# Relu² attention and a mixture-of-depths FFN on one core: batch 2's loads before the expert weights, and scatter-adds and row stores issued later

## Chip, cores and metric

The kernel runs on one core of a Trainium2 chip. The metric is the device time of one execution in microseconds, the median of the runs. The profile is of one further execution, whose span from the first to the last instruction was 249.8 us.

## What is computed

For 8 batches of 12 heads, 448 positions and head size 64, attention with a squared relu in place of softmax: `relu(q kᵀ / 8)² / 448` times `v`. The heads of a position, side by side, are its row `x` of 768 numbers. Then a gate `score = x · w_gate` picks the 128 highest positions of each batch, and only those rows go through a feed-forward layer:

```python
top_idx = np.argpartition(-scores[b], capacity)[:capacity]
xe = x[b, top_idx]
h = np.maximum(xe @ w1, 0.0)          # w1: 768 x 1024
ye = h @ w2                           # w2: 1024 x 768
g = 1.0 / (1.0 + np.exp(-scores[b, top_idx]))
out[b, top_idx] = x[b, top_idx] + g[:, None] * ye
```

All other rows of `out` are `x` itself. All inputs and the output are float32 in device memory; the kernel works in bfloat16.

## The kernel before

**Loop.** One loop runs over 48 steps `t`, one for each pair of heads; batch `b` has the six steps `hp` = 0 to 5. A step transposes q and k of the next pair on TensorE (`transposes`, L165 and L171; copied out by VectorE at L176), makes scores in four chunks (L186, L190), applies relu on ScalarE (L198) and squares on VectorE (L204), multiplies the step before with `v` (`attend`, L214), and copies that result to `xT` (`evacuate`, L223 or L225). From `xT` a DMA transpose on SyncE's queue (L229) fills `x_sb[b]`, the rows of the batch.

**The second half runs behind the first.** In batch `b` the steps also carry, for batch `b-1`, the gate scores and the ranking (`moe_rank`: scores L257, rank compare L280 against the constant `tie`, one-hot L285 against `slot_row`, gather L296), and, for batch `b-2`, the feed-forward layer (`moe_ffn`: h L329, y L345, the gated result `gye` L350). `chosen` (L305 to L307) copies the selected token numbers to the tile `idx`; for batch `b` it stands at the first step of batch `b+2`. `idx` and `gye` have two buffers each, `x_sb` two, the q, k and v buffers three.

**Order of work.** The loop stands under a manual schedule: each engine runs its instructions in the order in which the loop writes them. What stands ahead of the loop (first loads, constants) is placed by the scheduler, mostly in the order of the text.

**Transfers on GpSimd's (POOL's) queue.** All loads convert float32 to bfloat16 and are issued by GpSimd. `load(b)` is nine transfers: one of q (L79), four of k and four of v (L88, L91), together 4.1 MB read. Ahead of the loop come `load(0)` in parts, `load(1)`, three iotas that make `slot_row`, `tie` and the token numbers (L131, L137, L144), and the weights w1 and w2 (L152, L153; 3.1 MB each). Within the loop, `load(b+2)` stands at the first step of batch `b`; then the store of the rows of batch `b-1` (L233) follows from `evacuate`; and at the fifth-numbered step (`hp` = 5) `gated` calls the scatter-add of batch `b-2` (`scatter`, L384), an indirect DMA that adds 128 rows of `gye` into `out` at the positions in `idx`. Stores and scatter-adds of any batch write the same tensor `out`, and each of one kind waits for the one of the other kind issued before it.

Of the kernel before, what the change touches and what calls it, by code (L numbers as in the profile page):

```python
# [19 lines left out]
def kernel(  # L20
# [11 lines left out]
    nc = tc.nc  # L32

    B, H, S, Dh = q.shape
# [3 lines left out]
    P = 112  # L38
    NC = S // P
    NM = HD // 128  # L40
    NF = F // 128
    NHP = H // 2
# [52 lines left out]
    def load(b, h0, h1):  # L95
        load_q(b, h0, h1)
        load_kv(k_sb, k, b, h0, h1)
        load_kv(v_sb, v, b, h0, h1)
# [16 lines left out]
    for i in range(1, NBUF):  # L115
        zero_halves(i)
    load(1, 0, H)
    w1_sb = const.tile([128, NM, F], BF16)
    w2_sb = const.tile([128, NF, HD], BF16)

    wg_rep = const.tile([128, NM, 128], BF16)
    nc.vector.tensor_copy(out=wg_rep,
# [26 lines left out]
        nc.vector.tensor_copy(out=t[:, :, 0:2], in_=tok_i)  # L149
        tok.append(t)  # L150

    nc.gpsimd.dma_start(out=w1_sb, in_=moe_w1.rearrange("(m p) f -> p m f", p=128))  # L152
    nc.gpsimd.dma_start(out=w2_sb, in_=moe_w2.rearrange("(m p) f -> p m f", p=128))  # L153


    qkt, s_ps, a_sb, o_ps, x_sb = {}, {}, {}, {}, {}
# [43 lines left out]
    def square(t, c):  # L200
        n = 2 if c < 3 else 1
        r = r_sb.pop((t, c))
        a = a_sb[t, c] = a_pool.tile([128, 2, S], BF16, name="a_sb")
        nc.vector.tensor_tensor(out=a[:, :n], in0=r[:, :n], in1=r[:, :n], op=ALU.mult)  # L204
# [13 lines left out]
    def evacuate(t):  # L218
        b, hp = divmod(t, NHP)
        xt = xT[b % 2][:, hp, :, :P]  # L220
        o = o_ps.pop(t).rearrange("d (c p) -> d c p", p=P)
        if hp in (0, 4, 5):
            nc.vector.tensor_scalar(out=xt, in0=o, scalar1=o_scale, scalar2=None, op0=ALU.mult)  # L223
        else:
            nc.scalar.activation(out=xt, in_=o, func=AF.Copy, scale=o_scale)  # L225
        if hp == 0:
            x_sb[b] = x_pool.tile([128, NC, HD], BF16, name="x_sb")

        nc.sync.dma_start_transpose(  # L229
            out=x_sb[b][:, :, hp * 128:(hp + 1) * 128],  # L230
            in_=xT[b % 2][:, hp].rearrange("d c p -> d (c p)"))
        if hp == NHP - 1:
            nc.gpsimd.dma_start(out=out[b].rearrange("(p c) d -> p c d", c=NC), in_=x_sb[b][:P])  # L233

# [83 lines left out]
    def moe_ffn(b, idx, g, xeT):  # L320
        hT = moe_pool.tile([128, NF, CAP], BF16, name="hT")
        gye = moe_pool.tile([CAP, HD], FP32, name="gye")
        ps = {}

        def hidden(f, pool=mb_ps_pool, tag="m"):
            if f % 4 == 0:
                ps["h", f // 4] = pool.tile([128, 4, CAP], FP32, name="h_ps", tag=tag)
            for m in range(NM):
                nc.tensor.matmul(out=ps["h", f // 4][:, f % 4, :],  # L329
                                 lhsT=w1_sb[:, m, f * 128:(f + 1) * 128],  # L330
                                 rhs=xeT[:, m, :], start=(m == 0), stop=(m == NM - 1))

        def hidden_relu(i):
            nc.scalar.activation(out=hT[:, 4 * i:4 * i + 4, :], in_=ps["h", i], func=AF.Relu)

        def sigmoid():
            nc.scalar.activation(out=g, in_=g, func=AF.Sigmoid)

        def project(half, f0, f1, pool=None, tag="m"):
            cols_d = slice(half * 384, half * 384 + 384)  # L340
            if f0 == 0:
                pool = pool or (ma_ps_pool, mb_ps_pool)[half]
                ps["y", half] = pool.tile([CAP, 384], FP32, name="ye_ps", tag=tag)
            for f in range(f0, f1):
                nc.tensor.matmul(out=ps["y", half], lhsT=hT[:, f, :], rhs=w2_sb[:, f, cols_d],  # L345
                                 start=(f == 0), stop=(f == NF - 1))

        def gated(half):
            cols_d = slice(half * 384, half * 384 + 384)
            nc.scalar.activation(out=gye[:, cols_d], in_=ps["y", half], func=AF.Copy,  # L350
                                 scale=g[:, 0:1])
            if half == 1:
                scatter()

        def last():

            nc.scalar.activation(out=g, in_=g, func=AF.Sigmoid)
            for half in range(2):
                h = s_ps_pool.tile([128, 4, CAP], FP32, name="h_ps2", tag="s")
                for m0 in (0, 3):  # L360
                    for ff in range(4):
                        f = 4 * half + ff
                        for m in range(m0, m0 + 3):
                            nc.tensor.matmul(out=h[:, ff, :],
                                             lhsT=w1_sb[:, m, f * 128:(f + 1) * 128],
                                             rhs=xeT[:, m, :], start=(m == 0 and ff == 0),
                                             stop=(m == NM - 1), skip_group_check=True)
                f = 4 * half
                nc.scalar.activation(out=hT[:, f:f + 4, :], in_=h, func=AF.Relu)
            y = [mb_ps_pool.tile([CAP, 384], FP32, name="y_ps2", tag="m"),  # L370
                 t_ps_pool.tile([CAP, 384], FP32, name="y_ps3", tag="t")]
            for f0 in (0, 4):
                for half in range(2):
                    for f in range(f0, f0 + 4):
                        nc.tensor.matmul(out=y[half], lhsT=hT[:, f, :],
                                         rhs=w2_sb[:, f, half * 384:half * 384 + 384],
                                         start=(f == 0), stop=(f == NF - 1))
            nc.scalar.activation(out=gye[:, :384], in_=y[0], func=AF.Copy, scale=g[:, 0:1])
            nc.vector.tensor_scalar(out=gye[:, 384:], in0=y[1], scalar1=g[:, 0:1],
                                    scalar2=None, op0=ALU.mult)  # L380
            scatter()

        def scatter():
            nc.gpsimd.indirect_dma_start(  # L384
                out=out.rearrange("b s d -> (b s) d"),
                out_offset=bass.IndirectOffsetOnAxis(ap=idx[:, :1], axis=0),
                in_=gye, in_offset=None, element_offset=b * S * HD, compute_op=ALU.add)

        return {"h": hidden, "hT": hidden_relu, "sig": sigmoid, "y": project, "gye": gated,
                "last": last}  # L390


# [24 lines left out]
    def moe(engine, b, hp):  # L417

        if b >= 2 and hp == 0:
            place(engine, b - 1, NHP)  # L420
        place(engine, b, hp)
# [13 lines left out]
    with tc.manual_schedule():  # L435
        transposes(0)
        for t in range(NT):
            b, hp = divmod(t, NHP)
            scores(t, 0)
            scores(t, 1)  # L440
            relu(t, 0)
            relu(t, 1)
            moe(ACT, b, hp)
            if t > 0:
                square(t - 1, 3)
            moe(DVE, b, hp)
            if t + 1 < NT:
                transposes(t + 1)
            if t > 0:
                attend(t - 1)  # L450
                if hp not in (0, 1, 5):
                    evacuate(t - 1)
            if hp == 0 and b + 2 < B:
                load(b + 2, 0, H)
            scores(t, 2)
            relu(t, 2)
            square(t, 0)
            if t > 0 and hp in (0, 1, 5):
                evacuate(t - 1)
            square(t, 1)  # L460
            moe(DVE2, b, hp)
            scores(t, 3)
            relu(t, 3)
            square(t, 2)
            moe(PE, b, hp)
        square(NT - 1, 3)
        place(ACT, B - 1, NHP)
        place(DVE, B - 1, NHP)
        last, prev = B - 1, B - 2
        r, handed[last] = moe_rank(last)  # L470
        f = moe_ffn(prev, *handed.pop(prev))
        attend(NT - 1)
        evacuate(NT - 1)
        r["gate"](0, NM - 1)
        for i in range(4):
            f["h"](i)
        r["gate"](NM - 1, NM)
        f["hT"](0)
        r["bc"]()
        for i in range(4, 8):  # L480
            f["h"](i, t_ps_pool, "t")
        r["col"]()
        r["pieces"]()
        for c in range(NC):
            r["rank"](c)
        r["hot"]()
        f["hT"](1)
        f["sig"]()
        f["y"](0, 0, 8, mb_ps_pool)
        f["y"](1, 0, 8, o_ps_pool, "o")  # L490
        f["gye"](0)
        f["gye"](1)
        r["xe"](0, t_ps_pool, "t")
        r["sel"]()
        r["xe"](1, ma_ps_pool)
        r["xeT"](0)
        r["xeT"](1)
        r["chosen"]()
        moe_ffn(last, *handed.pop(last))["last"]()
# [33 lines left out]
```

## Time and profile before

| | |
|---|---|
| time, median of 3 | 253.89 us (253.05 to 253.95) |
| span of the profiled execution | 249.8 us |
| TensorE busy | 201.2 us, 81% |
| VectorE busy | 179.9 us, 72% |
| ScalarE busy | 183.2 us, 73% |
| GpSimd busy | 83.5 us, 33% |
| moved by DMA | 40.50 MB (39.32 MB read from device memory, 14.16 MB written to it) |
| mean granted TensorE clock | 0.942 |

The page has the busy time of each engine, then the span in 40 equal slices with a digit for the busy tenths in each, then the DMA queues, the chain of work that ended last, and the costliest groups of instructions. Lines of a timeline give start, duration (both in us), engine, source line, operation, output and input, the count, and in brackets the idle time before it and what ended that. For a DMA the engine's line is only its issue; the landing is seen in who waited for it. The median time from issue to landing was 10.8 us for the row stores (L233), 5.9 us for the scatter-adds (L384), 11.7 us for the q loads and 21.7 us for the weights.

### The profile page before, as it was taken

The numbers are of one execution on the slowest core, as the hardware profiler recorded it, in microseconds if no ns is written. First come the engines' busy times: TensorE is split into PE (matmuls) and PEld (weight loads), VectorE is DVE, ScalarE is ACT, GpSimd is POOL, SyncE is SP. The second block draws the span as 40 slices with busy tenths as digits, with TensorE's granted clock in tenths as the row PEclk, the third lists the DMA queues.
The fourth block names the chain that finished last, engine by engine and source line by source line (L and its number), as shares of the span: only waits on it lengthen the run. The fifth ranks groups of instructions, "written<-read, shape, count | busy, mean of one in ns | idle before, by whom it ended". The sixth has DMA issues, their size and how long they took to land.

```text
span 249.8 us, 5910 instructions
## 1 busy us (share of the span) xinstructions
PE 201.2 (81%) x2304; PEld 115.5 (46%) x2304; DVE 179.9 (72%) x430; ACT 183.2 (73%) x273; POOL 83.5 (33%) x117
## 2 busy tenths in 40 slices
PE   1677789730599979999999999999999499999730
PEld 0233244310265536654565456555655256456710
DVE  5274789960287979798979998998999289974300
ACT  2376989960078998899889979997999568964210
POOL 8998671101645410091101910092103012020220
PEclk9997999975589999999999999999999979999995
DMA  4999999999999999989998999999994968667443
GB/s 37 106 133 180 186 138 180 204 176 183 192 192 162 316 188 234 197 114 155 185 173 131 135 172 157 267 110 141 142 278 118 154 220 127 223 70 172 120 62 55
DMA packets 67692, 40.50 MB, mean 162 GB/s; under 512 B 40912, under 2 KB 64976, under 8 KB 66768
## 3 DMA queue, kind: packets, MB, share of 16 engines
q0 software_dynamic: 40768, 33.82, 84.4%
q1 hardware_dynamic: 26896, 6.30, 25.2%
q8 instruction: 18, 0.29, 0.5%
q14 instruction: 10, 0.08, 0.1%
HBM read 39.32 MB, written 14.16 MB: 214 GB/s over the span
## 4 chain that ended last, share of the span: by engine, by line
DMA 31%; PE 30%; ACT 12%; DVE 9%; POOL 8%; issue 6%; POOLq 1%; ACTq 0%; DVEq 0%
DMA k_sb<-in_k_dram 19%; ACT r_sb L198 9%; DMA q_sb<-in_q_dram 5%; PE s_ps L186 5%; PE o_ps L214 5%; DVE a_sb L204 4%; DMA out_dram<-x_sb 4%; PE xe_ps L296 4%; PE sc_ps L257 3%; PE h_ps L329 3%; DMA out_dram<-gye,idx 3%; PE ye_ps L345 2%; DVE trash L280 2%; PE t_ps L165 2%; PE s_ps L190 2%
## 5 line engine op out<-in xcount | busy, mean ns | idle before, releaser
L198 ACT ACTIVATE r_sb<-s_ps 128x896 bf16<-128x896 f32 x192 | 148.7, 833 | 41.9 <-PE s_ps L186 41.3
L204 DVE TENSOR_TENSOR a_sb<-r_sb 128x896 bf16<-128x896 bf16 x192 | 100.4, 559 | 10.5 <-ACT r_sb L198 9.4
L186 PE MATMUL s_ps<-qkt 64*128 64x448 bf16 x288 | 50.1, 368 | 11.4 <-ACT r_sb L198 9.3
L176 DVE COPY qkt<-t_ps 128x960 bf16<-128x960 bf16 x48 | 31.4, 654 | 31.4 <-PE t_ps L171 31.4
L214 PE MATMUL o_ps<-a_sb,v_sb 128*64 128x448 bf16 x384 | 47.7, 369 | 0.2 <-DVE a_sb L204 0.2
L384 POOL DMA_INDIRECT out_dram<-gye,idx x8 | 13.6, 1696 | 77.9 <-ACT r_sb L198 22.2
L186 PEld LDWEIGHTS <-qkt 64*128 64x128 bf16 x288 | 14.4, 94 | 46.7 <-issue 36.5
L165 PE MATMUL t_ps<-ident,q_sb 112*64 112x112 bf16 x384 | 19.6, 227 | 14.0 <-DMA q_sb<-in_q_dram 14.0
L91 POOL DMA_DIRECT2D v_sb<-in_v_dram x20 | 15.6, 780 | 42.5 <-DMA q_sb<-in_q_dram 22.8
L171 PE MATMUL t_ps<-ident,k_sb 128*64 128x128 bf16 x384 | 21.3, 230 | 6.2 <-DMA k_sb<-in_k_dram 6.2
L329 PE MATMUL h_ps<-xeT,w_sb 128*128 128x128 bf16 x336 | 22.1, 219 | 4.0 <-DVE xeT L311 3.1
L214 PEld LDWEIGHTS <-v_sb 128*64 128x64 bf16 x384 | 20.7, 115 | 9.0 <-issue 1.9
L165 PEld LDWEIGHTS <-q_sb 112*64 112x64 bf16 x384 | 12.1, 114 | 26.9 <-DMA q_sb<-in_q_dram 15.1
L329 PEld LDWEIGHTS <-w_sb 128*128 128x128 bf16 x336 | 20.4, 97 | 7.2 <-issue 5.7
L280 DVE SCALAR_TENSOR_TENSOR trash<-bc,cols,tie 112x448 bf16<-112x448 f32 x32 | 21.7, 678 | 0.1
L88 POOL DMA_DIRECT2D v_sb<-in_v_dram x20 | 17.1, 854 | 13.5 <-DMA w_sb<-in_moe_w_dram 9.0
L345 PE MATMUL ye_ps<-w_sb,hT 128*128 128x384 bf16 x112 | 20.3, 326 | 0.0
L91 POOL DMA_DIRECT2D k_sb<-in_k_dram x20 | 17.6, 885 | 2.2 <-PE s_ps L190 2.2
L190 PE MATMUL s_ps<-qkt 128*128 128x448 bf16 x48 | 17.7, 368 | 0.7 <-ACT r_sb L198 0.2
L171 PEld LDWEIGHTS <-k_sb 128*64 128x64 bf16 x384 | 14.7, 116 | 7.5 <-DMA k_sb<-in_k_dram 4.6
L88 POOL DMA_DIRECT2D k_sb<-in_k_dram x20 | 17.3, 870 | 0.2 <-issue 0.2
L223 DVE TENSOR_SCALAR xT<-o_ps 128x448 bf16<-128x448 f32 x24 | 14.8, 618 | 0.5 <-PE o_ps L214 0.5
(61 smaller groups left out, 176.1 us busy)
## 6 DMA issues: line engine op xcount, KB each, us to landing
out_dram<-x_sb POOLq DMA_DIRECT2D x8, 1344.0 KB, 10.8
q_sb<-in_q_dram POOLq DMA_DIRECT2D x7, 672.0 KB, 11.7
w_sb<-in_moe_w_dram POOLq DMA_DIRECT2D x2, 1536.0 KB, 21.7
k_sb<-in_k_dram POOLq DMA_DIRECT2D x14, 192.0 KB, 13.2
v_sb<-in_v_dram POOLq DMA_DIRECT2D x14, 192.0 KB, 10.4
k_sb<-in_k_dram POOLq DMA_DIRECT2D x14, 144.0 KB, 12.5
v_sb<-in_v_dram POOLq DMA_DIRECT2D x14, 144.0 KB, 14.2
x_sb<-xT SPq DMA_TRANSPOSE x48, 7.5
```

Of the source, the lines that this page charges most:

```text
L88: nc.gpsimd.dma_start(out=t[0:64, hs, 0:lo, :], in_=src[b, hs, 0:64 * lo].rearrange("h (p c) d -> p h c d", c=lo))
L91: nc.gpsimd.dma_start(out=t[64:128, hs, 0:hi, :], in_=src[b, hs, 64 * lo:S].rearrange("h (p c) d -> p h c d", c=hi))
L165: nc.tensor.matmul(out=ps[64 * hh:64 * hh + 64, c * P:(c + 1) * P], lhsT=qs[:, h0 + hh, c, :], rhs=ident[:P, :P], is_transpose=True, start ...
L171: nc.tensor.matmul(out=ps[64 * hh:64 * hh + 64, S + c * 128:S + (c + 1) * 128], lhsT=ks[:, h0 + hh, c, :], rhs=ident, is_transpose=True, s ...
L176: nc.vector.tensor_copy(out=sb, in_=ps)
L186: nc.tensor.matmul(out=ps[:, hh, :S], lhsT=sb[rows, S + c * 128:S + (c + 1) * 128], rhs=sb[rows, :S], start=True, stop=True)
L198: nc.scalar.activation(out=r[:, :n], in_=s_ps.pop((t, c))[:, :n, :S], func=AF.Relu)
L204: nc.vector.tensor_tensor(out=a[:, :n], in0=r[:, :n], in1=r[:, :n], op=ALU.mult)
L214: nc.tensor.matmul(out=o_ps[t][rows, :], lhsT=vs[:, 2 * hp + hh, c, :], rhs=a[:, hh if c < 3 else 0, :], start=(c == 0), stop=(c == 3), sk ...
L280: nc.vector.scalar_tensor_tensor(out=trash, in0=bc[:P, :], scalar=cols[:, c:c + 1], in1=tie[:, c, :], op0=ALU.subtract, op1=ALU.is_ge, acc ...
L329: nc.tensor.matmul(out=ps["h", f // 4][:, f % 4, :], lhsT=w1_sb[:, m, f * 128:(f + 1) * 128], rhs=xeT[:, m, :], start=(m == 0), stop=(m == ...
L345: nc.tensor.matmul(out=ps["y", half], lhsT=hT[:, f, :], rhs=w2_sb[:, f, cols_d], start=(f == 0), stop=(f == NF - 1))
```

## The change

Three edits. The loads of batch 2 are taken out of the loop and issued right behind those of batch 1, so that batch 2's q, k and v are in the queue before the weights. The issue of the weights is moved up to just behind them, ahead of the iotas. And the scatter-adds and row stores are no longer issued where their data comes out: both stand at the end of the third step (`hp` = 2) of a batch, the scatter-add of batch `b-3` first, then the store of batch `b-1`. The aim is that loads, which compute will need, do not stand behind weights that are needed later or behind writes that nobody is waiting for.

```diff
     load(1, 0, H)
+    load(2, 0, H)
     w1_sb = const.tile([128, NM, F], BF16)
     w2_sb = const.tile([128, NF, HD], BF16)
+    nc.gpsimd.dma_start(out=w1_sb, in_=moe_w1.rearrange("(m p) f -> p m f", p=128))
+    nc.gpsimd.dma_start(out=w2_sb, in_=moe_w2.rearrange("(m p) f -> p m f", p=128))
...
-    nc.gpsimd.dma_start(out=w1_sb, in_=moe_w1.rearrange("(m p) f -> p m f", p=128))
-    nc.gpsimd.dma_start(out=w2_sb, in_=moe_w2.rearrange("(m p) f -> p m f", p=128))
...
-        if hp == NHP - 1:
-            nc.gpsimd.dma_start(out=out[b].rearrange("(p c) d -> p c d", c=NC), in_=x_sb[b][:P])
+
+    def store(b):
+        nc.gpsimd.dma_start(out=out[b].rearrange("(p c) d -> p c d", c=NC), in_=x_sb[b][:P])
...
-            if half == 1:
-                scatter()
-
...
-            if hp == 0 and b + 2 < B:
+            if hp == 0 and 2 < b + 2 < B:
                 load(b + 2, 0, H)
...
             moe(PE, b, hp)
+            if hp == 2:
+                if b >= 3:
+                    ffn_steps[b - 3]["add"]()
+                if b >= 1:
+                    store(b - 1)
...
         evacuate(NT - 1)
+        ffn_steps[B - 3]["add"]()
+        store(last)
...
         f["gye"](1)
+        f["add"]()
```

More of the change, by code (lines that the diff above doesn't have):

```diff
@@ L387, in scatter @@
                 in_=gye, in_offset=None, element_offset=b * S * HD, compute_op=ALU.add)
-        return {"h": hidden, "hT": hidden_relu, "sig": sigmoid, "y": project, "gye": gated,
+        return {"h": hidden, "hT": hidden_relu, "sig": sigmoid, "y": project, "gye": gated, "add": scatter,
                 "last": last}
```

## The prediction, made before the changed kernel was run

> **What bounds the kernel now.** I read the slices of the page first, then the chain of waits in order of time, then GpSimd's (POOL's) timeline with what ended each wait, then VectorE's (DVE's). The slices:
>
> ```profile
> PE   1677789730599979999999999999999499999730
> DMA  4999999999999999989998999999994968667443
> ```
>
> A slice is 6.2 us. TensorE has two holes, slices 8 to 10 (about 53 to 66 us) and slice 31 (about 195 to 199). The DMA engines are 90% busy or more from slice 1 to slice 29, but for two at 8 (17 and 21). So until about 187 us the transfers are a limit of their own, just hidden behind compute, and a hole closed by reordering may only move. The chain confirms that both holes are transfers:
>
> ```profile
> 34.74 31.53 DMA k_sb<-in_k_dram
> ...
> 180.06 10.40 DMA out_dram<-x_sb
> ...
> 191.34 6.95 DMA out_dram<-gye,idx
> ```
>
> The first is batch 2's load, behind the weights in POOL's queue. What ended POOL's waits shows a queue served in order with eight transfers under way at most:
>
> ```profile
> 47.56 0.66 POOL L91 DMA_DIRECT2D v_sb<-in_v_dram  x1 [9.15 <-DMA w_sb<-in_moe_w_dram]
> 57.22 0.66 POOL L88 DMA_DIRECT2D v_sb<-in_v_dram  x1 [9.00 <-DMA w_sb<-in_moe_w_dram]
> ```
>
> These are the second and third v pieces of batch 2; each was released by the transfer issued eight before it: w1 landed at 47.4 us, w2 at 57.1. TensorE got q of batch 2 at 62.4 and the last of k at 66.4. It had wanted them at 53.0.
>
> The second hole is a buffer: idx has two, so the index of batch b can't be written before scatter-add b-2 has landed.
>
> ```profile
> 198.38 0.16 DVE L306 TENSOR_TENSOR idx<-sel 128x1 int32<-128x1 f32 x1 [4.50 <-DMA out_dram<-gye,idx]
> ```
>
> VectorE's queue is in order: behind L306 stand xeT, the next qkt copy and the squares, so TensorE and ScalarE (ACT) stop too. The rows of L306 begin at 71.0, 97.4, 121.5, 145.6, 169.8 and 198.4 us for batches 0 to 5: compute needs **24.2 us a batch**. The scatter-adds come later and later:
>
> ```profile
> 105.60 1.69 POOL L384 DMA_INDIRECT out_dram<-gye,idx  x1 [13.48 <-DVE a_sb L204]
> 106.69 1.66 POOL L79 DMA_DIRECT2D q_sb<-in_q_dram  x1
> ...
> 136.54 1.71 POOL L384 DMA_INDIRECT out_dram<-gye,idx  x1 [16.05 <-ACT xT L225]
> 137.68 1.60 POOL L79 DMA_DIRECT2D q_sb<-in_q_dram  x1
> ...
> 162.73 1.66 POOL L384 DMA_INDIRECT out_dram<-gye,idx  x1 [11.49 <-ACT r_sb L198]
> ```
>
> Scatters 0 to 3 start at 105.6, 136.5, 162.7 and 191.3: **28.6 us apart on average, more than compute's 24.2**. The releasers named had long been done. Each scatter waited for the row store ahead of it, since both write `out`; for the fourth the chain shows that store, ending at 190.5. Scatters 0, 1, 2 land about 9, 3 and 1 us before L306 needs them, scatter 3 is 4.5 late. The transfers are thus already nearly the bound.
>
> **What the Trainium skill says.** "DMA: Bandwidth & Descriptors", section "Queues, rings and completion order": every DMA engine takes turns, packet by packet, between the queue rows that have work; its section "Two DMAs through the same engine are not ordered" adds that descriptors within one queue of an engine start in order. The trace agrees: batch 2 came after the weights. All loads, weights, stores and scatters are on one queue (q0, 84.4% of the engines' span), the transposes on another (25.2%). Its "Rules for kernel authors" want an accumulating DMA to wait for the earlier DMA on the same bytes; that is the store-scatter chain. Its "Anatomy of one DMA" puts waits on the issuing engine, not on the DMA engines. POOL shows it: load 5's q is issued at 106.69, only after the scatter's wait.
>
> **The change, part by part.**
>
> *Batch 2 ahead of the weights.* Load 1 has landed by 36.9 (v at 37.05 waited for its last piece). Load 1 took 14.5 us beyond load 0 (q landed at 27.4, 5 us into it). So q of batch 2 lands at about 42, all of it at 51.5, w1 at 62, w2 at 72. Wanted at 53: the **13 us hole goes**. The first h matmuls stand 2.8 us behind L306 of batch 0 and now want w1 at 60 to 65; w2 is wanted 12 us later. A wait of up to 2 us.
>
> *The iotas* now stand behind w2's issue. w2 needs the transfer eight before it, the second k piece of batch 2, which lands at about 44; so the iotas run at 45 to 47 where they ran at 28 to 30. The rank compare that reads `tie` (45.14 now) stalls about 4 us, or up to 11 if VectorE's copies keep their place (36 us). I take 4. Load 3 lands at about 87 (72 plus 15), its k at 82, wanted at 80 to 84: 0 to 2 us. Batch 3 would begin some 8 us earlier than now. All three terms cost nothing, because the next step holds compute for longer.
>
> *Scatter first, half a batch later.* In POOL's order this is one swap. Before: scatter b-3, load b+2, store b-1. After: load b+2, scatter b-3, store b-1. The load no longer waits behind the scatter's wait. But the scatter now lands after the load in the queue, and L306 of batch b-1 still waits for it. Bytes are unchanged, and the set ahead of scatter 0 has grown by load 5:
> - Loads 0 to 4, weights and stores 0 and 1 had landed at 105.6. Same work, queue never empty: 105.
> - Load 5: load plus store took 24.0, 19.4 and 21.5 us in the three later cycles (112.5 to 136.5, 143.1 to 162.5, 169.0 to 190.5), mean 21.6; less 3.5 for the store (store 0 took 83.1 to 86.6) leaves 18. **123**.
> - Scatter 0: 5.5 to 7.0 us from issue to landing, here issued early, so without its 1.65 us of issue: 5. **128**, where compute free of waits would want it at about 113. L306 of batch 2 then runs at 128, not 121.5.
> - After that a cycle is store issue (about 1), store and load (21.6), scatter (5): 27.6 us. L306 of batch 3 at 155.6 (now 145.6), of batch 4 at 183.2 (now 169.8).
> - Batch 5 needs scatter 3, one store and one scatter after scatter 2, about 193, no load between. Compute sets it: 183.2 + 24.2 = **207.4, where it was 198.4: 9 us later**.
>
> A cross-check needs no cycle: loads 0 to 7, stores 0 to 3 and scatters 0 to 2, the set that must now land before L306 of batch 4, had in the old trace landed at about 187 (190.5 less a store; the slices' DMA digit falls to 4 at 187).
>
> *The tail* (end of scatter 3 on) has the same POOL order in both kernels: scatter, store, ..., store 7, scatter 6, scatter 7. I cost it at nothing: the work from L306 of batch 5 to the end, 51.4 us, comes behind compute as before. Transposes held by x_sb's two buffers wait for stores that land later (store 0 at about 91 instead of 86.6), but that row data is read a batch later.
>
> Sum: +9 us on 253.9, less about 1 for the restart after the old late hole: **262**.
>
> **Rivals.**
> - *A, forecast*, between the measured means: 256 to 269. Against it: the slow cycle of 24.0 may be peculiar to that stretch.
> - *B, the queue keeps compute's pace.* With the fastest load plus store seen (86.6 to 105.6, 19.0) and a scatter of 4: scatter 0 at 105 + 15.5 + 4 = 124.5; the cycle of 24 is under 24.2, so batch 5's L306 at 124.5 + 3 x 24.2 = 197.1: **252.6**, about no change, a few us less if bursts run still faster. For: stretches at 213 GB/s exist. Against: one in four, and scatter stretches move about 114.
> - *C, scatters don't queue behind a load.* Both holes go: 253.9 - 13.0 - 4.5 = **236**. For: only the change's early part acts. Against: stores and loads all keep order on q0, and no second GpSimd queue shows.
> - *D, slow bounds everywhere* (load 20.5, scatter 7, cycle 32; iotas at their worst are hidden even then): L306 of batch 4 at 197, **277**.
>
> **How the numbers follow.** A 0.72, B 0.17, C 0.06, D 0.05. B spreads from 250 to 255, about 0.09 faster, 0.07 the same, 0.01 slower. Faster 0.06 + 0.09 = 0.15, same 0.08, slower 0.77. Range 251 to 270: C, D, some of B's low end and A's rim stay outside, under 0.2.
>
> **What would show it.** Right: no hole at 53 to 66; one at roughly 113 to 128; L306 of batches 2, 3 and 4 released by the scatter, the first near 128, then 26 to 29 us apart; POOL order load, scatter, store; iotas near 46. Wrong: scatters landing within 7 us of issue while a load is under way (C), or L306 every 24.2 us after one stall (B). A hole longer than 4 us for w1 or load 3 would be a wait that I set too low.

## Result and the profile after

The changed kernel is slower. Its time is 271.04 us (median of 4, 265.31 to 273.74) beside 253.92 us before; the ratio is **1.052, 95% interval 1.039 to 1.065**. The ratio leaves out disturbed runs, so it stands for about 267 us rather than for the median of 271. The same kernel once more, in a later comparison (experiment 9), took 266.9 us beside 253.1.

| | before | after |
|---|---|---|
| span of the profiled execution, us | 249.8 | 263.5 |
| index write of batches 0 to 5 (before L306, after L308), us | 71.0, 97.4, 121.5, 145.6, 169.8, 198.4 | 62.8, 88.0, 129.9, 156.4, 186.0, 211.1 |
| waits of the index write for a scatter-add, us | 4.5 (once) | 26.4 (three times) |
| index write of batch 5 to the end, us | 51.4 | 52.4 |

The index write is the instruction that puts a batch's selected token numbers into `idx`. Lines of the changed kernel are numbered a little differently: the index write is L308, the row store L235, the scatter-add L383, the gated result L352. The page's slices, now 6.6 us each:

```profile
PE   1687498779989999940199989996699999998840
DMA  3999999999999999999499999999858367157424
```

TensorE's hole at 53 to 66 us is gone: the ninth and tenth slices have 7 and 9. In its place stands a longer one, the digits 4, 0 and 1 of the 18th to 20th slices (112 to 132 us), and two slices at 6 from 178 to 191 us. The DMA row is at 9 from 7 us on, with one dip to 4 (125 to 132 us, in which the 9 of the load gives way to the lone scatter-add), and thins out only from 185 us, when the last load has landed. VectorE's timeline, index writes of batches 2 to 5, the idle time ahead of each in brackets:

```profile
129.87 0.16 DVE L308 TENSOR_TENSOR idx<-sel 128x1 int32<-128x1 f32 x1 [17.79 <-DMA out_dram<-gye,idx]
...
156.43 0.16 DVE L308 TENSOR_TENSOR idx<-sel 128x1 int32<-128x1 f32 x1 [2.25 <-DMA out_dram<-gye,idx]
...
186.03 0.16 DVE L308 TENSOR_TENSOR idx<-sel 128x1 int32<-128x1 f32 x1 [6.35 <-DMA out_dram<-gye,idx]
...
211.11 0.16 DVE L308 TENSOR_TENSOR idx<-sel 128x1 int32<-128x1 f32 x1
```

The first three wait 17.8, 2.3 and 6.4 us for a scatter-add. The fourth waits for nothing: no load stands ahead of scatter-add 3. GpSimd's timeline, issues of scatter-add, store and q load:

```profile
117.88 1.70 POOL L383 DMA_INDIRECT out_dram<-gye,idx  x1 [1.35 <-DMA k_sb<-in_k_dram]
130.07 0.60 POOL L235 DMA_DIRECT2D out_dram<-x_sb  x1 [10.49 <-DMA out_dram<-gye,idx]
130.66 0.99 POOL L79 DMA_DIRECT2D q_sb<-in_q_dram  x1
...
146.52 1.67 POOL L383 DMA_INDIRECT out_dram<-gye,idx  x1 [0.87 <-DVE a_sb L205]
156.89 0.58 POOL L235 DMA_DIRECT2D out_dram<-x_sb  x1 [8.70 <-DMA out_dram<-gye,idx]
157.47 1.00 POOL L79 DMA_DIRECT2D q_sb<-in_q_dram  x1
...
193.58 1.85 POOL L383 DMA_INDIRECT out_dram<-gye,idx  x1 [6.76 <-DVE xT L224]
199.76 0.58 POOL L235 DMA_DIRECT2D out_dram<-x_sb  x1 [4.33 <-DMA out_dram<-gye,idx]
```

Scatter-adds 0 and 1 are issued at 117.9 and 146.5 and have landed by 129.8 and 156.3, when the store and the index write go on: about 12 and 10 us. Scatter-add 3, with no load ahead, lands 5.9 us after its issue (193.6 to 199.5). In the trace's semaphore records the last v piece of loads 5, 6 and 7 lands at 127.9, 153.8 and 184.5, and scatter-adds 0, 1, 2 behind them at 129.8, 156.3 and 185.9, always within 2.6 us. The scatter-add isn't slow; it stands behind 4.1 MB.

### The profile page after: what moved, and what is told of

It reads as the page before. It is cut to its first block, busy times and chain, and to the rows that moved or that the text cites. A ratio compares the mean times of both kernels' runs of the same rounds, so it can differ in the third digit from the quotient of the medians.

```text
span 263.5 us, 5909 instructions
## 1 busy us (share of the span) xinstructions
PE 205.3 (78%) x2304; PEld 117.1 (44%) x2304; DVE 179.6 (68%) x430; ACT 182.9 (69%) x273; POOL 82.9 (31%) x117
## 4 chain that ended last, share of the span: by engine, by line
PE 27%; DMA 26%; DVE 14%; ACT 10%; issue 10%; POOL 9%; POOLq 1%; ACTq 0%; DVEq 0%
DMA k_sb<-in_k_dram 18%; DMA out_dram<-gye,idx 9%; ACT r_sb L199 8%; DVE a_sb L205 6%; PE s_ps L187 5%; PE o_ps L215 4%; PE sc_ps L259 3%; PE xe_ps L298 3%; DVE trash L282 3%; PE h_ps L331 2%; POOL q_sb L79 2%; POOL k_sb L88 2%; DVE qkt L177 2%; PE t_ps L166 2%; POOL k_sb L91 2%
## 5 line engine op out<-in xcount | busy, mean ns | idle before, releaser
L331 PE MATMUL h_ps<-xeT,w_sb 128*128 128x128 bf16 x336 | 22.6, 222 | 21.8 <-DVE xeT L313 21.0
L187 PEld LDWEIGHTS <-qkt 64*128 64x128 bf16 x288 | 14.4, 94 | 47.5 <-issue 36.0
L331 PEld LDWEIGHTS <-w_sb 128*128 128x128 bf16 x336 | 20.8, 99 | 25.4 <-issue 24.1
L91 POOL DMA_DIRECT2D v_sb<-in_v_dram x20 | 13.5, 676 | 46.4 <-DMA q_sb<-in_q_dram 15.1
L383 POOL DMA_INDIRECT out_dram<-gye,idx x8 | 13.2, 1653 | 46.6 <-DVE a_sb L205 17.1
L88 POOL DMA_DIRECT2D v_sb<-in_v_dram x20 | 13.6, 680 | 21.1 <-DMA w_sb<-in_moe_w_dram 8.9
L166 PEld LDWEIGHTS <-q_sb 112*64 112x64 bf16 x384 | 12.2, 114 | 17.7 <-issue 11.7
L308 DVE TENSOR_TENSOR idx<-sel 128x1 int32<-128x1 f32 x8 | 1.3, 159 | 26.6 <-DMA out_dram<-gye,idx 26.4
L235 POOL DMA_DIRECT2D out_dram<-x_sb x8 | 4.6, 576 | 46.9 <-DMA out_dram<-gye,idx 34.8
L191 PE MATMUL s_ps<-qkt 128*128 128x448 bf16 x48 | 17.8, 372 | 0.7 <-ACT r_sb L199 0.2
L298 PE MATMUL xe_ps<-hot,x_sb 112*128 112x128 bf16 x192 | 13.2, 220 | 3.2 <-DVE hot L287 2.0
## 6 DMA issues: line engine op xcount, KB each, us to landing
v_sb<-in_v_dram POOLq DMA_DIRECT2D x14, 192.0 KB, 12.2
```

The source lines that it names most:

```text
L88: nc.gpsimd.dma_start(out=t[0:64, hs, 0:lo, :], in_=src[b, hs, 0:64 * lo].rearrange("h (p c) d -> p h c d", c=lo))
L166: nc.tensor.matmul(out=ps[64 * hh:64 * hh + 64, c * P:(c + 1) * P], lhsT=qs[:, h0 + hh, c, :], rhs=ident[:P, :P], is_transpose=True, start ...
L187: nc.tensor.matmul(out=ps[:, hh, :S], lhsT=sb[rows, S + c * 128:S + (c + 1) * 128], rhs=sb[rows, :S], start=True, stop=True)
L298: nc.tensor.matmul(out=xe[:, mm, :], lhsT=xb[:P, c, m * 128:(m + 1) * 128], rhs=hot[:, c, :], start=(c == 0), stop=(c == NC - 1))
L331: nc.tensor.matmul(out=ps["h", f // 4][:, f % 4, :], lhsT=w1_sb[:, m, f * 128:(f + 1) * 128], rhs=xeT[:, m, :], start=(m == 0), stop=(m == ...
```

## Experiments

Theory T: the scatter-add's place behind a load in the one GpSimd transfer queue, together with idx's two buffers, costs the time. The table has all runs; "index waits", the index write of batch 5 and the span are those of the profiled execution, and a dash stands where no ratio is on record.

| kernel | time, us (runs) | ratio to before | index waits, us | index write of batch 5 | span, us |
|---|---|---|---|---|---|
| 1 front part only | 256.6 (20) | 1.004 [0.999, 1.008] | 14.6 | 201.8 | 253.7 |
| 2 second part only | 259.7 (4) | 1.029 [1.017, 1.041] | 14.4 | 207.1 | 259.4 |
| 3 change, 4 index buffers | 257.1 (4) | – | 0 | 200.9 | 253.6 |
| 4 change, 3 row buffers | 266.0 (4) | – | 25.6 | 213.6 | 264.3 |
| 5 change, all buffers deeper | 251.5 (20) | 0.978 [0.970, 0.986] | 0 | 187.1 | 249.7 |
| 6 change, loads 5 to 7 left out | 246.6 (4) | 0.970 [0.961, 0.980] | 5.3 | 194.3 | 245.1 |
| 7 front part, 4 index buffers | 254.2 (20) | – | 0 | 190.7 | 250.4 |
| 8 before, 4 index buffers | 252.2 (5) | 0.972 [0.959, 0.985] | 0 | 200.6 | 254.2 |
| 9 change once more | 266.9 (6) | – | 21.0 | 209.0 | 261.0 |
| 10 change, scatter ahead of load | 253.9 (6) | – | 12.2 | 198.3 | 248.3 |
| 11 second part once more | 255.2 (8) | – | 11.9 | 207.1 | 257.7 |
| 12 as 5, stores grouped at the end | 250.1 (6) | – | 0 | 188.0 | 247.9 |

The kernel before had medians of 253.5 beside runs 1 to 8 and 253.1 beside 9 to 12, and its single executions ran from 245 to 263 us, so differences of two or three microseconds between medians decide nothing here.

### 1. The front part only

```diff
     load(1, 0, H)
+    load(2, 0, H)
...
+    nc.gpsimd.dma_start(out=w1_sb, ...)      # and w2; ahead of the iotas
...
-            if hp == 0 and b + 2 < B:
+            if hp == 0 and 2 < b + 2 < B:
```

> Only the front part of the change: batch 2's loads and the weights moved up, stores and scatter-adds where they were. Theory T (the scatter-add's place in the queue costs the time): POOL's old order keeps scatter ahead of the load; the hole at 53 to 66 us is gone, but scatters still come about 28 us apart behind the same transfers, so the index write of batch 5 stays near 198 us: 252 to 256 us, no gain. Rival F (the front part itself, weights and iotas behind more loads, costs the time): 262 to 270 us. Rival N (transfers aren't a bound, the early hole was pure loss): about 241 us.

256.6 us, ratio 1.004: no gain, as T had it, though the median lies 0.6 us above its range. The early hole goes (index write of batch 0 at 64.9 us in place of 71.0), and four later waits for scatter-adds, 14.6 us in all, take it back: batch 5 stands at 201.8 against 198.4. The scatter-adds have their old place here, ahead of the next load; scatter-add 0 starts late because store 1, which it waits for, lands at 113.4 us, where it was 104.6 before. Neither F nor N holds.

### 2 and 11. The second part only

```diff
-        if hp == NHP - 1:
-            nc.gpsimd.dma_start(out=out[b].rearrange(...), in_=x_sb[b][:P])
...
-            if half == 1:
-                scatter()
...
+            if hp == 2:
+                if b >= 3:
+                    ffn_steps[b - 3]["add"]()
+                if b >= 1:
+                    store(b - 1)
```

> Only the second part: stores and scatter-adds at the third step, scatter first; batch 2 stays behind the weights. Theory T: the index writes of batches 2, 3 and 4 wait for scatters that land behind a load, near 129, 156 and 185 us, as in the whole change, although the early hole of 13 us is back, because compute waits there anyway: 263 to 270 us. Rival F: 252 to 256 us, as before. Rival N: the early hole back on top of the loss, 276 us or more.

> Only the second part, once more, on the same chip as the whole change. Theory T as predicted (compute waits for the same scatters with or without the early hole): within 1% of the changed kernel. Rival S (the front part lets store 1 land later, 111 us against 104, and so costs time by itself once the scatters bind): 1.5 to 3% faster than the changed kernel, 256 to 261 us.

259.7 us and, once more, 255.2 beside 266.9 for the whole change on the same chip. In both profiles the index writes of batches 2 to 4 wait for scatter-adds, as T says (124.0, 151.5 and 181.8 us in the first), and batch 5 comes at 207.1, 8.7 us later than before. But the whole change is 11.7 us slower than this part in the second comparison, not within 1%. So T's claim that the front part is hidden behind the scatter-adds **failed**; S predicted the direction, though the part came out 4.4% faster, outside its 1.5 to 3%. S's reason shows in the traces: store 1 lands at 104.2 and 106.5 us here and at 111.3 and 109.8 with the front part. In all ten profiles of kernels with the front part it lands between 109.8 and 118.6 us, without it at 104.6 (before), 104.2, 106.5 and, in run 8, 117.8. So the front part goes with a late store 1, but something else can delay it too; what does was not tried. The profiles of whole and part differ by only 3 to 4 us in span (263.5 and 261.0 against 259.4 and 257.7). Run 11's profiled execution took 259.5 us, 4 us more than its median, and run 9's took 262.8, 4 us less, so these profiles understate the difference. The rest lies in executions without a trace and stays open; their mean granted clock was 0.89 to 0.92 for the whole and 0.91 to 0.94 for the part. In the trace of the changed kernel the clock reads 0.50 in the hole from 120 to 131 us, so longer holes would fit, but none of those executions shows them.

### 3. Four index buffers in the changed kernel

```diff
+    idx_pool = ctx.enter_context(tc.tile_pool(name="idxp", bufs=4))
...
-        idx = small.tile([CAP, 1], INT32, name="idx")
+        idx = idx_pool.tile([CAP, 1], INT32, name="idx")
```

> The whole change, with four buffers for the index tile in place of two and nothing else. Theory T: no wait of the index write for a scatter; the 26 us of holes at 112, 154 and 180 us go, and the next holder of a scatter, the two buffers of gye, gives ScalarE waits of 0 to 6 us at the fifth step of batches 4, 5, 6: 243 to 250 us, faster than before. Rival X (rows held by late stores, and the transposes behind them, are what costs): 263 to 271 us, no change.

257.1 us: ten microseconds of the loss go with index buffers of 512 bytes each, but it isn't faster than before. The wait moved to the next holder of a scatter-add. ScalarE's timeline, the gated result of batch 4, and TensorE's, the gather of batch 2's rows:

```profile
193.02 0.58 ACT L353 ACTIVATE gye<-ye_ps,g 128x384 f32<-128x384 f32 x1 [5.71 <-DMA out_dram<-gye,idx]
```

```profile
116.16 0.61 PE L299 MATMUL xe_ps<-hot,x_sb 112*128 112x128 bf16 x4 [2.52 <-DMA x_sb<-xT]
```

The first waited 5.7 us for scatter-add 2, which still has to read the gye buffer (the gated result of batch 3 waited 1.6 likewise); the second 2.5 us for rows that wait for x_sb. ScalarE's waits were in T's expectation, TensorE's was not, nor was the time: 243 to 250 us was wrong. The three waits, 9.8 us together, are part of what left batch 5 at 200.9 us, 2.5 us later than before.

### 4. Three row buffers

```diff
-    x_pool = ctx.enter_context(tc.tile_pool(name="x", bufs=2))
+    x_pool = ctx.enter_context(tc.tile_pool(name="x", bufs=3))
```

> The whole change, with three buffers for the rows x_sb in place of two. Transposes no longer wait for the store of two batches earlier. Theory T: the index waits stay and set the time, 263 to 271 us, within 1% of the changed kernel. Rival X: the loss goes, 255 us or less.

266.0 us with index waits of 25.6 us: as the changed kernel. The held rows are not what the index write waits for. One of the four executions took 257.8 us, below every one of the changed kernel (262.8 to 273.7); it has no trace, so that the rows cost something besides is not excluded.

### 5. All buffers deeper

Four index buffers, four gye buffers and three row buffers: edits 3 and 4 together, and

```diff
+    gye_pool = ctx.enter_context(tc.tile_pool(name="gyep", bufs=4))
...
-        gye = moe_pool.tile([CAP, HD], FP32, name="gye")
+        gye = gye_pool.tile([CAP, HD], FP32, name="gye")
```

> The whole change with four index buffers, four gye buffers and three row buffers: everything a late scatter-add or store was seen to hold. With four index buffers alone the index write no longer waited, but gye did (1.6 and 5.7 us) and the gather for its rows (2.5). Theory T: those go too, 244 to 252 us. Rival P (the transfers themselves are the bound after about 140 us, whoever waits for them): batch 7's load or a piece of k comes late instead, 253 to 258 us.

251.5 us: faster than the changed kernel. Whether it is faster than the kernel before is less sure: the ratio is 0.978 [0.970, 0.986], but the medians of all executions lie only 2.0 us apart, and the profiled spans are equal (249.7 and 249.8). From batch 1 to batch 6 compute now runs without a hole: the index writes of batches 1 to 6 come at 90.4, 114.6, 138.8, 162.9, 187.1 and 211.1 us, 24.1 apart, and batch 5 stands 11 us ahead of the kernel before. Yet at most about two of these reach the end. GpSimd's issues of scatter-add 2 and store 4, and below them the chain of waits, in order of time:

```profile
177.30 1.79 POOL L385 DMA_INDIRECT out_dram<-gye,idx  x1 [0.78 <-ACT g L341]
189.62 0.59 POOL L237 DMA_DIRECT2D out_dram<-x_sb  x1 [10.53 <-DMA out_dram<-gye,idx]
```

```profile
196.18 6.50 DMA out_dram<-gye,idx
...
202.97 5.37 DMA out_dram<-x_sb
...
216.53 5.18 DMA out_dram<-x_sb
...
222.95 5.65 DMA out_dram<-gye,idx
...
228.89 5.20 DMA out_dram<-x_sb
...
234.90 5.50 DMA out_dram<-gye,idx
```

From 196 us on it is scatter-add and store in turn (the turn of scatter-add 4, issued at 209.2, stands in this view as time without a releaser), each issued only when the one before has landed, 6.4 us a turn over the nine turns from store 4's issue at 189.6 us to the last landing at 246.8. VectorE's last result is ready at 230 us. So a second bound lay right behind the first, and neither T nor P named it: the writes to `out` in turn. In the kernel before it was already as close: VectorE's last result was ready at 240.4 us, the scatter-add before the last had landed at 240.2, and the last landed at 246.9.

The loads still set when these turns begin. Scatter-adds 0 to 2, each behind a load, land at 132.1, 159.6 and 189.3 us, 27.5 and 29.7 apart; in the changed kernel it was 26.6 and 29.6. Deeper buffers did not make the queue faster; compute no longer waits for it. P had that part right, but no load or piece of k came late.

### 6. No loads for batches 5 to 7

```diff
-            if hp == 0 and 2 < b + 2 < B:
+            if hp == 0 and 2 < b + 2 < 5:
```

> The whole change, buffers as in it, with the loads of batches 5, 6 and 7 left out (those batches compute on the data of batches 2, 3 and 4). POOL's order of scatters and stores and all buffers stay. Theory T: with no load ahead of it, a scatter lands 6 to 7 us after its issue and well before its index write; no hole at 112 us, compute every 24.2 us from 88 us, the index write of batch 5 at 184 to 188: 236 to 242 us. A rival by which the scatter-add itself, its place in the program or the order scatter-store costs the time: 255 us or more still.

246.6 us. The index writes of batches 2 to 5:

```profile
121.52 0.16 DVE L308 TENSOR_TENSOR idx<-sel 128x1 int32<-128x1 f32 x1 [5.30 <-DMA out_dram<-gye,idx]
...
146.01 0.16 DVE L308 TENSOR_TENSOR idx<-sel 128x1 int32<-128x1 f32 x1
...
170.15 0.16 DVE L308 TENSOR_TENSOR idx<-sel 128x1 int32<-128x1 f32 x1
...
194.29 0.16 DVE L308 TENSOR_TENSOR idx<-sel 128x1 int32<-128x1 f32 x1
```

One wait of 5.3 us, then compute's 24.1 to 24.5 us a batch; scatter-adds take 5.5 to 7.2 us from issue to landing in the same program order and buffers. That is T's mechanism. Leaving the loads out also takes 12.4 MB off the queue, so this run alone does not tell the place behind a load from the load itself; run 10 does, with the same bytes. The time is 5 us above its range because store 1 landed at 113.5 us, not at the 105 on which the expectation stood, so scatter-add 0 began there.

### 7 and 8. Four index buffers without the second part

Edit 3 on the kernel of run 1, and on the kernel before.

> Only the front part of the change, with four index buffers. With two it had four waits of the index write, 14.6 us together, and no gain in time. Theory T: they go, nothing else holds a scatter (gye's next writer comes 35 us after it), and what is left is batch 7's load, which starts only behind a scatter's wait near 165 us: a hole of 0 to 8 us near 180: 241 to 248 us. Rival P (transfers bound whoever waits): 251 us or more.

> The kernel before with four index buffers and nothing else. It lost 4.5 us to the index write of batch 5. Theory T: that goes, the hole at 53 to 66 us stays: 247 to 251 us. Rival P: something else on the same transfers is late by as much, 252 to 255 us.

254.2 us for the first: compute gets ahead (batch 5 at 190.7 us against 201.8 in run 1), but the end comes from the same turns of store and scatter-add, the last landing at 247.4. T's 241 to 248 failed here for the reason that run 5 shows. The second has 252.2 us (246.1 to 256.1), in P's range and not in T's, and a ratio under 1, but the two medians lie 1.3 us apart; I take it as at best a small gain.

### 10. The scatter-add ahead of the load

```diff
+            if hp == 0 and b >= 3:
+                ffn_steps[b - 3]["add"]()
             if hp == 0 and 2 < b + 2 < B:
                 load(b + 2, 0, H)
...
             if hp == 2:
-                if b >= 3:
-                    ffn_steps[b - 3]["add"]()
                 if b >= 1:
                     store(b - 1)
```

> The whole change with one line moved: the scatter-add of batch b-3 stands at the first step, ahead of load b+2, and no longer behind it at the third; the store stays at the third step. Theory T (its place behind the load costs the time): scatters land 5.5 to 7 us after issue, index waits fall to 15 us or less, 252 to 258 us. Rival L (issuing writes half a batch later is what costs, in whatever order): within 1% of the changed kernel, 262 us or more.

> The changed kernel itself once more, beside the next three on one chip. All theories: three index waits, near 130, 156 and 186 us, 24 to 28 us in total: 262 to 271 us.

253.9 us beside 266.9 for the changed kernel on the same chip and 253.1 before. One line moved takes back the loss, as far as these runs tell, though stores are still issued half a batch later; L is out. The index writes of batches 2 to 5 in this kernel, and below them GpSimd's issues of scatter-add, load and store:

```profile
119.35 0.16 DVE L308 TENSOR_TENSOR idx<-sel 128x1 int32<-128x1 f32 x1 [5.48 <-DMA out_dram<-gye,idx]
...
144.82 0.16 DVE L308 TENSOR_TENSOR idx<-sel 128x1 int32<-128x1 f32 x1 [2.08 <-DMA out_dram<-gye,idx]
...
171.37 0.16 DVE L308 TENSOR_TENSOR idx<-sel 128x1 int32<-128x1 f32 x1 [2.83 <-DMA out_dram<-gye,idx]
...
198.28 0.16 DVE L308 TENSOR_TENSOR idx<-sel 128x1 int32<-128x1 f32 x1 [1.81 <-DMA out_dram<-gye,idx]
```

```profile
112.26 1.81 POOL L383 DMA_INDIRECT out_dram<-gye,idx  x1 [19.67 <-DVE xT L224]
113.47 1.65 POOL L79 DMA_DIRECT2D q_sb<-in_q_dram  x1
...
127.41 0.55 POOL L235 DMA_DIRECT2D out_dram<-x_sb  x1 [0.42 <-DMA x_sb<-xT]
...
138.03 1.65 POOL L383 DMA_INDIRECT out_dram<-gye,idx  x1 [10.07 <-ACT r_sb L199]
```

The four waits add up to 12.2 us. Scatter-add 0 is issued at 112.3 and lands at 119.3; the index write follows at 119.35, ten microseconds earlier than with a load ahead of it.

### 12. Stores grouped at the end

```diff
-                if b >= 3:
+                if 3 <= b <= 5:
                     ffn_steps[b - 3]["add"]()
                 if b >= 1:
                     store(b - 1)
+                if b == B - 1:
+                    ffn_steps[b - 4]["add"]()
+                    ffn_steps[b - 3]["add"]()
```

> The version with four index, four gye and three row buffers, and after the last load the stores 4, 5 and 6 ahead of scatter-adds 3 and 4, so that stores follow each other without a scatter between. With the buffers alone compute had no hole, yet the end came from nine writes in turn, store, scatter, store, some 6.4 us each from 189 to 247 us. Theory C (that chain of waits on out sets the end): two turns fewer, 5 to 10 us less than the version with the buffers alone, 241 to 247 us. Rival: compute sets the end, no change, 249 to 252 us.

250.1 us against 251.5 for run 5, spans 247.9 and 249.7: in the expected direction, too little to tell from nothing. Stores 4 and 5 were issued back to back at 186.9 and 187.6, but store 6's rows were not there before 198.2, and six turns still follow it. The size of C's forecast failed; that the chain sets the end in this kernel too is what its last scatter-add shows, issued at 239.5, when the one before it had landed. A version in which writes of different batches don't wait for each other was not tried.

## Why the prediction was right, and where it was off

- **Direction and mechanism: right.** The step that carried the forecast was the swap in GpSimd's order. It put L306 of batches 2, 3, 4 and 5 at 128, 155.6, 183.2 and 207.4 us; they ran at 129.9, 156.4, 186.0 and 211.1 (129.1, 156.0, 184.6 and 209.0 in run 9). Runs 10 and 6 took away the load ahead of the scatter-add by order and by omission, and the long waits went.
- **Size: 262 forecast, about 267 measured.** In the profile batch 5 is 12.7 us late where 9 were forecast: 1.9 from scatter-add 0, 1.0 from the two cycles (26.6 and 29.6 us for 27.6), 0.9 from the last batch (25.1 for 24.2). The tail took 1.0 more, where the sum had taken off 1. The executions that were only timed are longer than the profiled one by 3.5 to 8.4 us, in run 9 by 1.9 to 8.6.
- **"Same work, queue never empty: 105" was mis-sized.** Store 1 landed at 111.3. That it hardly shows is luck: load 5 took 16.6 us where 18 were put, and a scatter-add already in the queue landed 1.4 to 2.6 us behind the load where 5 were put. The estimate subtracted only the issue from the 5.5 to 7 us of a lone scatter-add; most of the rest of its latency was hidden too. The cycle of 27.6 is close by the same luck: the short scatter-adds made up for store and load, which took 23.7 and 27.7 us where 22.6 were put. The cross-check by the set of transfers needed no such luck: 187 forecast, 185.9 landed.
- **"All three terms cost nothing" failed.** The front part doesn't pay alone (run 1), but with the second part it isn't free: run 11 is 11.7 us faster than the whole by the medians, 3.4 in the profiles. The step took compute's wait as fixed by the second part; the landing that the wait starts from moved as well.
- **The terms at the front.** The iotas ran at 45.4 to 47.4 us as forecast, and the 4 us stall didn't come: VectorE's copy of them stands at 49.5 us. Instead TensorE waited 2.6 us for k of batch 1, which the forecast didn't have. w1 landed at 58.5 and w2 at 68.1 us, and no compute engine waited for them; GpSimd's issue of two v pieces of batch 3 did, for 6.6 and 8.9 us.
- **The rivals.** C is out: scatter-adds do queue behind loads. B's pace of 24 us a cycle didn't come, nor D's of 32. The bound that lay next was in the prediction only as "the tail, costed at nothing": true for the changed kernel, where compute sets the end, and the reason why the repaired kernels gain about 2% at best and not 5.
- **A reading of the chain of writes.** The prediction explains the waits between stores and scatter-adds by a rule for writes to the same bytes. The waits that count here are between different batches: scatter-add 3 waited for store 4, whose rows are others. The kernel waits because both write the tensor `out`. The forecast doesn't rest on the reason, only on the waits.

## What to carry to other kernels

On a queue that is served in order, ask of each transfer not when its data is wanted in memory but which buffer it holds until it lands, and who rewrites that buffer: a write that "nobody waits for" still held a 512-byte index tile, and through it VectorE. When an order is changed to bring loads forward, deepen first what the delayed writes hold, and look for the next chain before counting the gain; here it was the alternation of writes to one tensor at the end. In this case each hole closed while the transfers stayed 90% busy came back elsewhere: the early one at the index write, that one at the end (run 5: batch 5 is 11 us ahead of the kernel before, the span the same).

## What was not expected of the hardware

The sixteen DMA engines that share a transfer can finish far apart. In the trace of before they reported store 1 between 103.1 and 104.6 us. In the changed kernel fifteen had reported by 105.7, and the last came at 111.3. For the two v pieces of load 4 ahead of that store, too, the last report came 5.1 us after the other fifteen (at 103.8 and 108.0); the counts don't say whether it was the same engine each time. In other runs with the front part there is no single late one: the reports of store 1 spread from 104.6 to 113.4 us in run 1 and from 103.3 to 113.5 in run 6. What waits for a transfer waits for its last report: in the changed kernel the v piece of load 5 that waited for store 1 was issued at 111.55 us, right behind the sixteenth. What sets the spread was not tried. And a scatter-add queued behind a load landed 1.4 to 2.6 us after it in the changed kernel, where alone it takes 5.5 to 7 us from issue to landing.
